# Stacked attention scores: head by head in five one-bank rounds, and earlier due times for the copies of the stacked parts

## The chip, the cores and the metric

One core of one Trainium2 chip runs the whole program. The metric is device time in microseconds of one execution; lower is better. Three runs of the kernel before gave 959.68, 962.39 and 964.31 us (median 962.39).

## The reference

Three layers follow one another, all in float32:

```python
# attention: q, k, v are [8 batches, 8 heads, 576, 64]; mask by blocks of 64
scores = q @ k.T / 8;  scores[block_i < block_j] = -1e9
attn = exp(scores - rowmax);  attn /= rowsum + 1e-9
x = (attn @ v)                     # -> [4608 tokens, 512]
# first layer: h = x @ w_in [512 x 2048];  g = h if h > 0 else exp(h) - 1;  x = g @ w_out
# second layer: logits = x @ phi [512 x 32]; softmax over tokens dispatches to 8 experts,
# softmax over slots combines their outputs -> [4608, 512]
```

Row block u of 128 queries needs only the keys 0 to 128(u+1), so a head has score pieces that are 128, 256, 384 and 512 wide, and a last one of 64 queries by 576 keys.

## The kernel before, in words

**Work.** The two heads of one batch that stand side by side are a pair: 32 pairs (`NPAIR`), four to a batch. The tokens form 36 tiles of 128. While pairs of later batches go through attention, tiles of earlier ones go through the layers (`moe_tile`: 48 matmuls L861 to L863 of 512 columns for a tile, then transposes by way of DRAM, `turned`, and routing, L906 and L972). Pairs from 9 on (`STACK`) use the stacked form that the change is about, 23 of them; they run between 215 and 760 us of the span.

**A stacked pair.** q and k come in transposed by 32x32 blocks and DVE finishes the turn (L532) into `QT[0]` and `KT[0]`, of which there is one copy. `pair_split` makes each head's stacked operands: ACT rounds q into `X1` (L555) and k into `Y` (L557), POOL forms the rests `KL` (L561) and `X2` (L566), and two DMAs a head copy `X1` and `KL` to the other 64 partitions (`qk_late<-qk_late`, four a pair). Operands of a head are one buffer, so those of the next pair wait for this pair's score matmuls.

**Scores.** `pair_scores` makes one fill after another in the two PSUM banks `SB0` and `SB0+512`. Piece `"b"` (the last 64 queries of both heads, L602) lies across both banks. Pieces `(u, h)` of row block u and head h go to bank h. Fill 1 is `(3,0)` and `(3,1)`, fill 2 `(2,0)`, `(0,0)` and `(2,1)`, `(0,1)`, fill 3 `(1,0)` and `(1,1)`: six bank loads a pair (L621). For each, DVE writes the mask (L629, L631) and takes the row maximum (L634), and ACT takes exp with the row sum (L637) into an SBUF area; that empties the bank.

**After the scores.** A pair is normalized in two halves, `HALVES`: `"b"` with fill 1, and fills 2 and 3. `pair_weights` takes the reciprocals (L649, L650) and POOL scales the pieces (L654). `pair_swap` transposes them: part by PE (L368) and part by DVE (L736), which then go to DRAM as one store (`swapped<-att`) and come back in six loads (`att<-swapped`). `swapped_values` multiplies by v (L786).

**What sets the order.** Every operation is given to `Plan.add` with an engine, an estimated duration, what it reads and writes, and a due time (`key`). `Plan.order` simulates the engines with these estimates, and on each engine takes the ready operation with the lowest key. What comes out is a fixed order for each engine; at run time each queue is followed strictly, and semaphores make it wait. Reads and writes are tracked there by named keys, while the framework below it also orders two engines' accesses to one PSUM bank in the order in which they were written out. SyncE (SP) issues all DMAs of this stretch from one queue (L363); the plan counts 0.48 us for each issue. Keys that matter here, with `base` the due time of a pair, 24 apart within a batch: scores `base + 4 fl`, halves of the weights and their swap `base + 7` and `base + 16`, loads of q and k `base - 30`, of v `base - 16`, preparation `base - 14` and some more. `turned` traffic of tile i has `22 i + 5.5 r + 0.5`.

Of the kernel before, what the change touches and what calls it, by code (L numbers as in the profile page):

```python
# [18 lines left out]
P = 128  # L19
# [15 lines left out]
MASKED = -1e9  # L35
# [204 lines left out]
def attention_moe_kernel(ctx: ExitStack, tc, q, k, v, w_in, w_out, phi, w1, w2, consts, out):  # L240
# [74 lines left out]
    def f(o, n, p0=0, p1=P):  # L315
        return view(as_f32, o, n, p0, p1)
# [7 lines left out]
    def pb(o, n, p0=0, p1=P):  # L324
        return ps[p0:p1, o:o + n]
# [218 lines left out]
    def pair_split(n, key):  # L544


        add("POOL", 0.64, lambda e: nc.gpsimd.tensor_scalar(
            out=f(QT[0], 512), in0=f(QT[0], 512), scalar1=SCALE, scalar2=0.0, op0=ALU.mult, op1=ALU.add), w=[("qt", 0)], key=key + 0.5)
        for h in range(2):
            here, there = (D * h, D * h + D), (D - D * h, P - D * h)  # L550
            x1, x2, y, kl = X1[h], X2[h], Y[h], KL

            def key_of(j):
                return [("stack", h, j)]
            add("ACT", 0.5, lambda e, x1=x1, here=here: nc.scalar.copy(st(x1, 512, *here), f(QT[0], 512, *here)),  # L555
                r=[("qt", 0)], w=key_of(0), key=key + 1)
            add("ACT", 0.5, lambda e, y=y, here=here: nc.scalar.copy(st(y, 512, *here), f(KT[0], 512, *here)),  # L557
                r=[("kt", 0)], w=key_of(1), key=key + 1)
            load(lambda x1=x1, there=there: st(x1, 512, *there, F32), lambda x1=x1, here=here: st(x1, 512, *here, F32), 200000,
                 r=key_of(0), w=key_of(2), key=key + 2, lag=TLAG)  # L560
            add("POOL", 1.35, lambda e, y=y, here=here: nc.gpsimd.tensor_tensor(  # L561
                out=st(KL, 512, *here), in0=f(KT[0], 512, *here), in1=st(y, 512, *here, F32), op=ALU.subtract),
                r=[("kt", 0)] + key_of(1), w=[("kl", h)], key=key + 2)
            load(lambda y=y, there=there: st(y, 512, *there, F32), lambda here=here: st(KL, 512, *here, F32), 200000,
                 r=[("kl", h)], w=key_of(3), key=key + 3, lag=TLAG)
            add("POOL", 1.47, lambda e, x1=x1, x2=x2, here=here: nc.gpsimd.tensor_tensor(  # L566
                out=st(x2, 512, *here), in0=f(QT[0], 512, *here), in1=st(x1, 512, *here, F32), op=ALU.subtract),
                r=[("qt", 0)] + key_of(0), w=key_of(4), key=key + 3)
# [3 lines left out]
    FILLS = (("b",), ((3, 0), (3, 1)), ((2, 0), (2, 1), (0, 0), (0, 1)), ((1, 0), (1, 1)))  # L572
    HALVES = (FILLS[0] + FILLS[1], FILLS[2] + FILLS[3])

    def pat(x, n):

        return PB + (PW[0] * (n % 2) + UNITS[x][1] if x in HALVES[0] else PW[0] + UNITS[x][1])

    def pkey(x, n):
        return ("p", x, n % 2 if x in HALVES[0] else 0)  # L580

    def wide(x):
        return S if x == "b" else P * (x[0] + 1)

    def pair_scores(n, fill, key):
        s = n % 2
        one = s if n < STACK else 0
        qt, kt = QT[one], KT[one]
        banks, bkeys = ((H0, H0 + 512), [("h", 0), ("h", 1)]) if n < 4 and fill % 2 else ((SB0, SB0 + 512), [("sb", 0), ("sb", 1)])
        units = FILLS[fill]  # L590

        def at(x):
            return banks[0] + 224 if x == "b" else banks[x[1]] + (384 if x[0] == 0 else 0)

        def keys(x):
            return bkeys if x == "b" else [bkeys[x[1]]]

        def sc(e):
            if fill == 0 and n >= STACK:
# [12 lines left out]
        cols = S if fill == 0 else sum(wide(x) for x in units) // 2  # L612
        last = fill == 0 and n >= STACK
        if n >= STACK and not last:
            for h in range(2):
                mine = [u for u, y in units if y == h]

                def st_sc(e, h=h, mine=mine):
                    for u in mine:
                        for x, first in ((X1, True), (X2, False)):  # L620
                            mm(pb(at((u, h)), P * (u + 1)), lhsT=st(x[h] + P * u, P), rhs=st(Y[h], P * (u + 1)), start=first, stop=not first)  # L621
                add("PE", sum(2 * (0.016 + P * (u + 1) / 2400) for u in mine), st_sc, r=[("stack", h, j) for j in range(6)], w=[bkeys[h]], key=key)
        else:
            add("PE", (0.0 if last else 0.15) + cols / 600, sc, r=([("qb", s, h) for h in range(3)] if last else [("qt", one)]) + [("kt", one)],
                w=bkeys, key=key, load=1.0, mode="F" if last else "R")
        for x in units:
            if n >= STACK and fill == 2 and x[0] == 2:
                both = pb(at(x) + 256, 256, 0, 64).rearrange("p (a y) -> p a y", a=2)[:, :, 64:]
                add("DVE", 0.14, lambda e, both=both: nc.vector.memset(both, MASKED), w=keys(x), key=key)  # L629
            elif x != "b" and not (n >= STACK and fill == 2):  # L630
                add("DVE", 0.11, lambda e, x=x: nc.vector.memset(pb(at(x) + P * x[0] + 64, 64, 0, 64), MASKED), w=keys(x), key=key)  # L631
        for x in units:
            c = nm_col + 9 * s + UNITS[x][0]
# [3 lines left out]
            add("ACT", 0.50 + wide(x) / 1300, lambda e, x=x, c=c: nc.scalar.activation(  # L637
                f(pat(x, n), wide(x)), pb(at(x), wide(x)), AF.Exp, bias=f(c, 1), scale=1.0,
                accum_out=f(sum_col + 9 * s + UNITS[x][0], 1)),
                r=keys(x) + [("nm", s, x)], w=[pkey(x, n), ("sum", s, fill // 2)], key=key)  # L640

    def pair_weights(n, half, key):
        s = n % 2
        units = HALVES[half]
        c0, nc_ = UNITS[units[0]][0], len(units)
        sm, rs = sum_col + 9 * s + c0, rs_col + 9 * s + c0

        def rec(e):
# [3 lines left out]
        for x in units:  # L652
            p = pat(x, n)
            add("POOL", (0.28 + wide(x) / 1050) * (1.3 if n < 8 else 1.0), lambda e, x=x, p=p: nc.gpsimd.tensor_scalar(  # L654
                out=f(p, wide(x)), in0=f(p, wide(x)), scalar1=f(rs_col + 9 * s + UNITS[x][0], 1), scalar2=0.0,
                op0=ALU.mult, op1=ALU.add), r=[("rs", s, half)], w=[pkey(x, n)], key=key)

        if n >= NTP:
# [65 lines left out]
    def pair_swap(n, half, key):  # L724
# [5 lines left out]
        for x in HALVES[half]:  # L730
# [9 lines left out]
        groups = ([("b", c) for c in range(4)], [((3, 0), 3), ((3, 1), 3), ("b", 4)]) if half == 0 else ([((0, 0), 0), ((0, 1), 0)],)  # L740
        for gi, blocks in enumerate(groups):
            g = gi + 2 * half
            tb, tk = (PVB, "pvb")
# [4 lines left out]
            add("PE", 0.02 + 0.108 * len(blocks), tr, r=[pkey(x, n) for x in {b[0]: 0 for b in blocks}] + ["con"], w=[tk], key=key, load=0.0)  # L748

            def evac(e, g=g, tb=tb):  # L750
                if g == 0:
# [269 lines left out]
    def tail(key):  # L1021
        qkk = [("stack", h, j) for h in range(2) for j in range(6)] + [("kl", h) for h in range(2)]
        att = [(nm, a) for nm in ("rq", "rk") for a in range(4)] + [(nm, 0) for nm in ("qt", "kt")] + [("qb", s, h) for s in range(2) for h in range(3)] + \
              [("v", s, j) for s in range(NV) for j in range(3)] + [pkey(x, s) for x in UNITS for s in range(2)] + \
# [223 lines left out]
    for n in range(NPAIR):  # L1248
        b, p = divmod(n, 4)
        base = T * 4.5 * (b - 1) + 24.0 * p - 24.0 - (min(EARLY, 8.0 + 4.0 * (n - NTP)) if n >= NTP else 0.0) if b else KAS * p + KA0  # L1250
        ev.append((base - (27 if n < STACK else KLD) if n < STACK else max(base - KLD, free + 0.1), lambda n=n, x=base - KLD: pair_load(n, x)))
        ev.append((before + 12.1 if n >= STACK else base - 14, lambda n=n, x=base - 14: pair_prep(n, x)))
        free = before + 12.1 if n >= STACK else base + 24 if n < NTP else free
        before = base
        ev.append((base - 16, lambda n=n, x=base - 16: pair_load_v(n, x)))
        for fl in range(4):
            ev.append((base + 4 * fl, lambda n=n, fl=fl, x=base + 4 * fl: pair_scores(n, fl, x)))
        for h in range(2):
            ev.append((base + 9 * h + 7, lambda n=n, h=h, x=base + 9 * h + 7: pair_weights(n, h, x)))
        ev.append((max(base + 24, T * 4.5 * (b - 1) + 0.1 if n >= NTP else -1e9), lambda n=n, x=base + 24: pair_values(n, x)))  # L1260
# [46 lines left out]
```

## Time and profile before

| | |
|---|---|
| median of 3 runs | 962.39 us |
| the profiled execution, its own time | 961.83 us |
| its span (first to last instruction) | 960.0 us |
| PE busy | 904.3 us (94%) |
| DVE busy | 693.4 us (72%) |
| ACT busy | 497.6 us (52%) |
| POOL busy | 392.5 us (41%) |
| mean granted TensorE clock | 0.989 |
| share of the chain that ended last | PE 59%, DVE 11%, DMA 11%, SP queue 7%, ACT 4%, POOL 3%, issue 3% |

An engine's busy time is the union of its instructions, so what is missing to the span is idle time. The chain that ended last is followed back from the last instruction, at each step to what released it. "a <- b" in a list of waits means that a stood idle and b's end let it go.

### The profile page before, as it was taken

What the parts mean: (1) busy time and instruction counts of PE and PEld (TensorE: products, weight loads), DVE (VectorE), ACT (ScalarE), POOL (GpSimd) and SP (SyncE); (2) the same over time, 40 slices, a digit from 0 to 9 for tenths busy, and PEclk for the clock granted to TensorE, in tenths of its full rate; (3) what the DMA queues carried; (4) which work ended last, traced back from release to release, by engine and by line L of the source; (5) the groups of instructions that cost most, each with busy time, mean ns of one, the idle gap of its engine ahead of it and who ended that gap; (6) DMA issues with size and microseconds to landing.
All of it is one profiled execution on the core that took longest, in us unless ns stands there. A gap on an engine that the chain in (4) does not pass through costs nothing.

```text
span 960.0 us, 20080 instructions
## 1 busy us (share of the span) xinstructions
PE 904.3 (94%) x6817; PEld 654.8 (68%) x6817; DVE 693.4 (72%) x1677; ACT 497.6 (52%) x1375; POOL 392.5 (41%) x519
## 2 busy tenths in 40 slices
PE   8898999999999999999999999999999999999992
PEld 6566777667676776776777777777777776766351
DVE  5896795578987897887879888788898844333150
ACT  5784655565555655555555555645555433322143
POOL 2874342147644555454635554455556210000000
PEclk9999999999999999999999999999999999999996
DMA  9946765248888887888977788878886788058959
GB/s 237 251 127 174 217 192 174 68 118 217 218 235 222 219 239 208 230 218 217 238 217 218 205 216 228 226 209 227 230 229 203 238 299 300 1 202 306 370 217 352
DMA packets 258551, 209.19 MB, mean 218 GB/s; under 512 B 182417, under 2 KB 205585, under 8 KB 255377
## 3 DMA queue, kind: packets, MB, share of 16 engines
q1 hardware_dynamic: 257248, 207.61, 75.0%
q8 instruction: 55, 0.90, 0.4%
q10 hardware_dynamic: 1200, 0.30, 0.1%
q14 instruction: 48, 0.39, 0.1%
HBM read 125.52 MB, written 70.25 MB: 204 GB/s over the span
## 4 chain that ended last, share of the span: by engine, by line
PE 59%; DVE 11%; DMA 11%; SPq 7%; ACT 4%; POOL 3%; issue 3%; ACTq 0%; DVEq 0%; POOLq 0%
PE ps L861 10%; PE ps L863 9%; PE ps L862 9%; PE ps L368 7%; SPq L363 7%; PE ps L786 4%; PE ps L621 4%; POOL att L654 3%; DMA att<-swapped 3%; PE ps L972 3%; PE ps L906 2%; PE ps L815 2%; DVE base L634 2%; ACT att L637 2%; PE ps L610 2%
## 5 line engine op out<-in xcount | busy, mean ns | idle before, releaser
L654 POOL TENSOR_SCALAR att<-att,base 128x128 f32<-128x128 f32 (+4 forms) x288 | 183.4, 654 | 197.6 <-DVE base L650 120.0
L861 PE MATMUL ps<-w,xhl 128*128 128x512 f32 x576 | 247.4, 430 | 0.0
L637 ACT ACTIVATE att<-ps,base 128x128 f32<-128x128 f32 (+4 forms) x288 | 157.7, 552 | 139.5 <-DVE base L634 124.7
L863 PE MATMUL ps<-w,xhl 128*128 128x512 f32 x576 | 226.8, 394 | 0.6 <-POOL xhl L843 0.6
L862 PE MATMUL ps<-w,xhl 128*128 128x512 f32 x576 | 225.8, 392 | 0.0
L634 DVE TENSOR_REDUCE base<-ps 128x1 f32<-128x128 f32 (+4 forms) x288 | 138.0, 502 | 17.5 <-PE ps L606 10.8
L861 PEld LDWEIGHTS ps<-w,xhl 128*128 128x128 f32 x576 | 108.8, 189 | 32.8 <-issue 14.4
L863 PEld LDWEIGHTS ps<-w,xhl 128*128 128x128 f32 x576 | 108.1, 188 | 25.9 <-POOL xhl L843 1.2
L862 PEld LDWEIGHTS ps<-w,xhl 128*128 128x128 f32 x576 | 109.0, 189 | 14.1
L344 ACT COPY att<-ps 128x512 f32<-128x512 f32 (+3 forms) x184 | 73.2, 437 | 64.5 <-PE ps L368 59.4
L566 POOL TENSOR_TENSOR qk_late<-att,qk_late 64x512 fp32r<-64x512 f32 x46 | 61.1, 1328 | 89.2 <-ACT qk_late L555 57.2
L786 PE MATMUL ps<-att 128*64 128x128 f32 (+2 forms) x960 | 74.5, 308 | 8.2 <-DMA att<-swapped 5.5
L621 PE MATMUL ps<-qk_late 128*128 128x512 f32 (+3 forms) x368 | 78.3, 328 | 2.3 <-ACT att L637 1.6
L843 POOL TENSOR_TENSOR xhl<-xe,xhl 128x512 fp32r<-128x512 f32 x36 | 46.6, 1296 | 82.6 <-ACT xhl L841 82.5
L368 PE MATMUL ps<-base,att 128*128 128x128 f32 x416 | 69.5, 279 | 10.0 <-POOL att L654 9.4
L621 PEld LDWEIGHTS ps<-qk_late 128*128 128x128 f32 x368 | 61.7, 188 | 22.2 <-ACT att L637 7.6
L786 PEld LDWEIGHTS ps<-att 128*64 128x64 f32 x960 | 49.6, 140 | 37.3 <-issue 26.6
L368 PEld LDWEIGHTS ps<-base,att 128*128 128x128 f32 x416 | 49.3, 142 | 36.0 <-POOL att L654 15.9
L736 DVE STREAM_TRANSPOSE att<-att 128x384 f32<-128x384 f32 x144 | 68.9, 502 | 0.5 <-POOL att L654 0.5
L868 DVE TENSOR_SCALAR g<-g 128x512 f32<-128x512 f32 x80 | 46.5, 581 | 28.9 <-ACT g L866 28.6
L866 ACT ACTIVATE g<-ps 128x512 f32<-128x512 f32 x80 | 47.4, 596 | 35.5 <-PE ps L863 33.5
L561 POOL TENSOR_TENSOR qk_late<-att,qk_late 64x512 fp32r<-64x512 f32 x46 | 60.2, 1308 | 2.3 <-ACT qk_late L557 1.1
(159 smaller groups left out, 1464.5 us busy)
## 6 DMA issues: line engine op xcount, KB each, us to landing
turned<-g SPq DMA_DIRECT2D x60, 512.0 KB, 3.4
swapped<-att SPq DMA_DIRECT2D x24, 1024.0 KB, 4.8
qk_late<-qk_late SPq DMA_DIRECT2D x92, 128.0 KB, 3.1
g<-turned SPq DMA_DIRECT2D x120, 96.0 KB, 2.7
att<-swapped SPq DMA_DIRECT2D x48, 192.0 KB, 4.0
att<-in_v_dram SPq DMA_DIRECT2D x64, 128.0 KB, 3.6
g<-in_moe_w_in_dram SPq DMA_DIRECT2D x16, 512.0 KB, 5.6
att<-in_moe_w_dram SPq DMA_DIRECT2D x8, 1024.0 KB, 10.2
```

What stands on the lines that cost most here:

```text
L344: nc.scalar.copy(o, i)
L363: (nc.sync if e == "SP" else nc.scalar).dma_start(out=o() if callable(o) else o, in_=i() if callable(i) else i)
L368: mm(o, lhsT=i, rhs=f(IDN + base, n, base, base + n), start=True, stop=True, is_transpose=True)
L621: mm(pb(at((u, h)), P * (u + 1)), lhsT=st(x[h] + P * u, P), rhs=st(Y[h], P * (u + 1)), start=first, stop=not first)
L634: add("DVE", 0.08 + wide(x) / 960, lambda e, x=x, c=c: nc.vector.tensor_reduce(out=f(c, 1), in_=pb(at(x), wide(x)), axis=AX.X, op=ALU.max, ...
L637: add("ACT", 0.50 + wide(x) / 1300, lambda e, x=x, c=c: nc.scalar.activation(f(pat(x, n), wide(x)), pb(at(x), wide(x)), AF.Exp, bias=f(c, ...
L654: add("POOL", (0.28 + wide(x) / 1050) * (1.3 if n < 8 else 1.0), lambda e, x=x, p=p: nc.gpsimd.tensor_scalar(out=f(p, wide(x)), in0=f(p, w ...
L736: add("DVE", 0.12 + P * cs / 960, lambda e, x=x, o=o, cs=cs: nc.vector.transpose(out=o, in_=f(pat(x, n), P * cs).rearrange("p (c m i) -> p ...
L786: mm(pb(o, w, 64 * h, 64 * h + 64), lhsT=f(vs + 320 * h + D * c, D), rhs=rhs(h), start=start, stop=stop)
L861: mm(pb(bank, 512), lhsT=fr(xh + P * kk, P), rhs=hi, start=(kk == 0), stop=False)
L862: mm(pb(bank, 512), lhsT=fr(xh + P * kk, P), rhs=lo, start=False, stop=False)
L863: mm(pb(bank, 512), lhsT=fr(xl + P * kk, P), rhs=hi, start=False, stop=(kk == 3))
```

## The change

The pairs from 9 on get a layout of their own. Pieces go head by head in five rounds after `"b"`, each in one bank, the banks in turn: `(3,0)`; `(2,0)` with `(0,0)`; `(1,0)` with `(1,1)`; `(3,1)`; `(2,1)` with `(0,1)`. Each round waits only for the stacked operands of the heads that it uses. The due times of the rounds are 4, 5.5, 8, 9.5 and 12 after `base`. The first half is now `"b"` and the first two rounds, the second half the last three. `(1,0)` and `(1,1)` lie beside each other in one bank and get one mask instruction instead of two. The transposes by PE are grouped to fit (still three groups of 4, 3 and 2 blocks). The due times of the two copies of a head go from `key + 2` and `key + 3` to `key - 8`. Preparation of the next pair is entered at 13.1 instead of 12.1 after `base`, behind the last round.

```diff
@@ pair_split
             load(lambda x1=x1, there=there: st(x1, 512, *there, F32), lambda x1=x1, here=here: st(x1, 512, *here, F32), 200000,
-                 r=key_of(0), w=key_of(2), key=key + 2, lag=TLAG)
+                 r=key_of(0), w=key_of(2), key=key - 8, lag=TLAG)
...
             load(lambda y=y, there=there: st(y, 512, *there, F32), lambda here=here: st(KL, 512, *here, F32), 200000,
-                 r=[("kl", h)], w=key_of(3), key=key + 3, lag=TLAG)
+                 r=[("kl", h)], w=key_of(3), key=key - 8, lag=TLAG)
@@
+    UNITS2 = {"b": (0, 0), (3, 0): (1, 640), (2, 0): (2, 1152), (0, 0): (3, 1536), (1, 0): (4, 1664), (1, 1): (5, 1920),
+              (3, 1): (6, 2176), (2, 1): (7, 2688), (0, 1): (8, 3072)}
+    FILLS2 = (("b",), ((3, 0),), ((2, 0), (0, 0)), ((1, 0), (1, 1)), ((3, 1),), ((2, 1), (0, 1)))
+    HALVES2 = (FILLS2[0] + FILLS2[1] + FILLS2[2], FILLS2[3] + FILLS2[4] + FILLS2[5])
@@ pair_scores
+        late = n >= STACK
+        units = FILLS2[fill] if late else FILLS[fill]
+        mine = (fill - 1) % 2
 
         def at(x):
+            if late and x != "b":
+                return banks[mine] + (384 if x[0] == 0 else 256 if x == (1, 1) else 0)
...
-            for h in range(2):
-                mine = [u for u, y in units if y == h]
-
-                def st_sc(e, h=h, mine=mine):
-                    for u in mine:
-                        for x, first in ((X1, True), (X2, False)):
-                            mm(pb(at((u, h)), P * (u + 1)), lhsT=st(x[h] + P * u, P), rhs=st(Y[h], P * (u + 1)), start=first, stop=not first)
-                add("PE", ..., st_sc, r=[("stack", h, j) for j in range(6)], w=[bkeys[h]], key=key)
+            def st_sc(e):
+                for u, h in units:
+                    for x, first in ((X1, True), (X2, False)):
+                        mm(pb(at((u, h)), P * (u + 1)), lhsT=st(x[h] + P * u, P), rhs=st(Y[h], P * (u + 1)), start=first, stop=not first)
+            add("PE", ..., st_sc,
+                r=[("stack", h, j) for h in sorted({y for _, y in units}) for j in range(6)], w=[bkeys[mine]], key=key)
...
-            elif x != "b" and not (n >= STACK and fill == 2):
+            elif late and x == (1, 0):
+                both = pb(at(x), 512, 0, 64).rearrange("p (a y) -> p a y", a=2)[:, :, 192:]
+                add("DVE", 0.14, lambda e, both=both: nc.vector.memset(both, MASKED), w=keys(x), key=key)
+            elif x != "b" and not (late and (x[0] == 0 or x == (1, 1))):
@@ pair_swap
+            groups = ([("b", c) for c in range(4)], [((0, 0), 0), ((3, 0), 3), ("b", 4)]) if half == 0 else ([((0, 1), 0), ((3, 1), 3)],)
@@ the events
-        ev.append((before + 12.1 if n >= STACK else base - 14, lambda n=n, x=base - 14: pair_prep(n, x)))
+        ev.append((before + 13.1 if n >= STACK else base - 14, lambda n=n, x=base - 14: pair_prep(n, x)))
...
-        for fl in range(4):
-            ev.append((base + 4 * fl, lambda n=n, fl=fl, x=base + 4 * fl: pair_scores(n, fl, x)))
+        for fl in range(4 if n < STACK else 6):
+            x = base + (4 * fl if n < STACK else (0, 4, 5.5, 8, 9.5, 12)[fl])
+            ev.append((x, lambda n=n, fl=fl, x=x: pair_scores(n, fl, x)))
```

## Rows read from the trace of the kernel before

**Rows 1.** Busy time by stretch: stretch, length, PE, PEld, DVE, ACT, POOL, clock, DMA

```profile
560.00:660.00 100.00, 94.99 (x689) 72.78 (x682) 82.67 (x207) 53.31 (x152) 50.59 (x69) 0.98 0.82 222
660.00:760.00 100.00, 99.78 (x750) 76.12 (x751) 86.32 (x222) 55.95 (x164) 52.98 (x69) 1.00 0.79 218
sum 545.00, PE 525.90 PEld 399.33 DVE 463.04 ACT 303.59 POOL 292.34; mean PE 87.65 PEld 66.56 DVE 77.17 ACT 50.60 POOL 48.72
...
900.00:960.00 60.00, 40.33 (x303) 19.25 (x295) 17.58 (x28) 21.82 (x42) 0.00 (x0) 0.85 0.83 305
```

**Rows 2.** Waits of PE, 205 to 790 us: us in total, times, longest

```profile
PE ps L786 <- DMA att<-swapped: 5.5, 5, 1.8
PE ps L368 <- ACT base L949: 4.0, 3, 2.0
PE ps L786 <- DMA g<-turned: 2.5, 2, 1.8
PE ps L368 <- ACT base L942: 1.7, 1, 1.7
PE ps L906 <- DMA g<-turned: 1.7, 2, 1.1
PE ps L621 <- ACT att L637: 1.6, 3, 1.2
...
PE ps L621 <- DMA qk_late<-qk_late: 0.4, 1, 0.4
```

**Rows 3.** Groups by line and form, 205 to 790 us: busy, mean ns, idle before

```profile
L634 DVE TENSOR_REDUCE base<-ps 128x1 f32<-128x256 f32 x48 | 18.9, 409 | 0.4
...
L634 DVE TENSOR_REDUCE base<-ps 128x1 f32<-128x128 f32 x48 | 12.4, 273 | 3.3 <-ACT att L637 3.1
...
L631 DVE MEMSET ps<- 64x64 f32 x95 | 10.2, 112 | 13.7 <-PE ps L621 12.2 <-ACT g L866 0.5
...
L629 DVE MEMSET ps<- 64x128 f32 x46 | 7.5, 165 | 6.0 <-PE ps L621 3.6 <-ACT att L637 1.8
```

**Rows 4.** PE in order of time, around the scores of three pairs: start, length

```profile
300.09 0.64 PE L621 MATMUL ps<-qk_late 128*128 128x256 f32 x4
300.56 0.40 PE L861 MATMUL ps<-w,xhl 128*128 128x512 f32 x1
...
304.65 1.13 PE L602 MATMUL ps<-att 128*128 128x288 f32 x4
...
312.72 1.17 PE L621 MATMUL ps<-qk_late 128*128 128x512 f32 x4
...
346.20 0.40 PE L621 MATMUL ps<-qk_late 128*128 128x256 f32 x2
346.44 0.40 PE L861 MATMUL ps<-w,xhl 128*128 128x512 f32 x1
```

**Rows 5.** ACT, POOL and SP in order of time, preparation of one pair

```profile
300.45 0.62 ACT L555 CAST qk_late<-att 64x512 fp32r<-64x512 f32 x1 [0.63 <-issue]
...
309.75 0.74 ACT L637 ACTIVATE att<-ps,base 128x576 f32<-128x576 f32 x1 [1.25 <-DVE base L634]
...
302.41 2.64 POOL L561 TENSOR_TENSOR qk_late<-att,qk_late 64x512 fp32r<-64x512 f32 x2
...
303.75 2.85 SPq L363 DMA_DIRECT2D att<-swapped  x6
306.70 1.12 SPq L363 DMA_DIRECT2D qk_late<-qk_late  x2
...
308.54 1.64 SPq L363 DMA_DIRECT2D qk_late<-qk_late  x2
```

**Rows 6.** DMA issues of the page: count, size, us to landing

```profile
qk_late<-qk_late SPq DMA_DIRECT2D x92, 128.0 KB, 3.1
```

**Rows 7.** ACT and DVE in order of time, two pieces of one bank

```profile
319.43 0.58 ACT L637 ACTIVATE att<-ps,base 128x384 f32<-128x384 f32 x1 [0.57 <-POOL att L654]
...
320.13 0.95 DVE L634 TENSOR_REDUCE base<-ps 128x1 f32<-128x128 f32 x3 [0.63 <-ACT att L637]
```

More of the change, by code (lines that the diff above doesn't have):

```diff
@@ L573, in attention_moe_kernel, with units_of, halves_of @@
     HALVES = (FILLS[0] + FILLS[1], FILLS[2] + FILLS[3])
+    UNITS2 = {"b": (0, 0), (3, 0): (1, 640), (2, 0): (2, 1152), (0, 0): (3, 1536), (1, 0): (4, 1664), (1, 1): (5, 1920),
+              (3, 1): (6, 2176), (2, 1): (7, 2688), (0, 1): (8, 3072)}
+    FILLS2 = (("b",), ((3, 0),), ((2, 0), (0, 0)), ((1, 0), (1, 1)), ((3, 1),), ((2, 1), (0, 1)))
+    HALVES2 = (FILLS2[0] + FILLS2[1] + FILLS2[2], FILLS2[3] + FILLS2[4] + FILLS2[5])
+    def units_of(n):
+        return UNITS if n < STACK else UNITS2
+    def halves_of(n):
+        return HALVES if n < STACK else HALVES2
     def pat(x, n):
-        return PB + (PW[0] * (n % 2) + UNITS[x][1] if x in HALVES[0] else PW[0] + UNITS[x][1])
+        o = units_of(n)[x][1]
+        return PB + (PW[0] * (n % 2) + o if x in halves_of(n)[0] else PW[0] + o)
     def pkey(x, n):
-        return ("p", x, n % 2 if x in HALVES[0] else 0)
+        return ("p" if n < STACK else "p2", x, n % 2 if x in halves_of(n)[0] else 0)
     def wide(x):
@@ L586, in pair_scores @@
         s = n % 2
+        if n == STACK and fill == 0:
+            for m in range(2):
+                handover([pkey(x, STACK + m) for x in HALVES2[0]], [pkey(x, STACK + m - 2) for x in HALVES[0]])
+            handover([pkey(x, STACK) for x in HALVES2[1]], [pkey(x, STACK - 1) for x in HALVES[1]])
         one = s if n < STACK else 0
@@ L589, in pair_scores @@
         banks, bkeys = ((H0, H0 + 512), [("h", 0), ("h", 1)]) if n < 4 and fill % 2 else ((SB0, SB0 + 512), [("sb", 0), ("sb", 1)])
-        units = FILLS[fill]
+        late = n >= STACK
+        units = FILLS2[fill] if late else FILLS[fill]
+        mine = (fill - 1) % 2
         def at(x):
+            if late and x != "b":
+                return banks[mine] + (384 if x[0] == 0 else 256 if x == (1, 1) else 0)
             return banks[0] + 224 if x == "b" else banks[x[1]] + (384 if x[0] == 0 else 0)
         def keys(x):
-            return bkeys if x == "b" else [bkeys[x[1]]]
+            return bkeys if x == "b" else [bkeys[mine if late else x[1]]]
         def sc(e):
@@ L614, in pair_scores @@
         if n >= STACK and not last:
-            for h in range(2):
-                mine = [u for u, y in units if y == h]
-                def st_sc(e, h=h, mine=mine):
-                    for u in mine:
-                        for x, first in ((X1, True), (X2, False)):
-                            mm(pb(at((u, h)), P * (u + 1)), lhsT=st(x[h] + P * u, P), rhs=st(Y[h], P * (u + 1)), start=first, stop=not first)
-                add("PE", sum(2 * (0.016 + P * (u + 1) / 2400) for u in mine), st_sc, r=[("stack", h, j) for j in range(6)], w=[bkeys[h]], key=key)
+            def st_sc(e):
+                for u, h in units:
+                    for x, first in ((X1, True), (X2, False)):
+                        mm(pb(at((u, h)), P * (u + 1)), lhsT=st(x[h] + P * u, P), rhs=st(Y[h], P * (u + 1)), start=first, stop=not first)
+            add("PE", sum(2 * (0.016 + P * (u + 1) / 2400) for u, _ in units), st_sc,
+                r=[("stack", h, j) for h in sorted({y for _, y in units}) for j in range(6)], w=[bkeys[mine]], key=key)
         else:
@@ L626, in pair_scores @@
         for x in units:
-            if n >= STACK and fill == 2 and x[0] == 2:
+            if late and x != "b" and x[0] == 2:
                 both = pb(at(x) + 256, 256, 0, 64).rearrange("p (a y) -> p a y", a=2)[:, :, 64:]
                 add("DVE", 0.14, lambda e, both=both: nc.vector.memset(both, MASKED), w=keys(x), key=key)
-            elif x != "b" and not (n >= STACK and fill == 2):
+            elif late and x == (1, 0):
+                both = pb(at(x), 512, 0, 64).rearrange("p (a y) -> p a y", a=2)[:, :, 192:]
+                add("DVE", 0.14, lambda e, both=both: nc.vector.memset(both, MASKED), w=keys(x), key=key)
+            elif x != "b" and not (late and (x[0] == 0 or x == (1, 1))):
                 add("DVE", 0.11, lambda e, x=x: nc.vector.memset(pb(at(x) + P * x[0] + 64, 64, 0, 64), MASKED), w=keys(x), key=key)
         for x in units:
-            c = nm_col + 9 * s + UNITS[x][0]
+            c = nm_col + 9 * s + units_of(n)[x][0]
             add("DVE", 0.08 + wide(x) / 960, lambda e, x=x, c=c: nc.vector.tensor_reduce(
@@ L638, in pair_scores @@
                 f(pat(x, n), wide(x)), pb(at(x), wide(x)), AF.Exp, bias=f(c, 1), scale=1.0,
-                accum_out=f(sum_col + 9 * s + UNITS[x][0], 1)),
-                r=keys(x) + [("nm", s, x)], w=[pkey(x, n), ("sum", s, fill // 2)], key=key)
+                accum_out=f(sum_col + 9 * s + units_of(n)[x][0], 1)),
+                r=keys(x) + [("nm", s, x)], w=[pkey(x, n), ("sum", s, fill // (3 if late else 2))], key=key)
     def pair_weights(n, half, key):
         s = n % 2
-        units = HALVES[half]
-        c0, nc_ = UNITS[units[0]][0], len(units)
+        units = halves_of(n)[half]
+        c0, nc_ = units_of(n)[units[0]][0], len(units)
         sm, rs = sum_col + 9 * s + c0, rs_col + 9 * s + c0
@@ L654, in pair_weights @@
             add("POOL", (0.28 + wide(x) / 1050) * (1.3 if n < 8 else 1.0), lambda e, x=x, p=p: nc.gpsimd.tensor_scalar(
-                out=f(p, wide(x)), in0=f(p, wide(x)), scalar1=f(rs_col + 9 * s + UNITS[x][0], 1), scalar2=0.0,
+                out=f(p, wide(x)), in0=f(p, wide(x)), scalar1=f(rs_col + 9 * s + units_of(n)[x][0], 1), scalar2=0.0,
                 op0=ALU.mult, op1=ALU.add), r=[("rs", s, half)], w=[pkey(x, n)], key=key)
@@ L729, in pair_swap @@
             handover(swap_keys(0) + swap_keys(1), [x for y in range(NPT) for x in pt_keys[y]])
-        for x in HALVES[half]:
+        for x in halves_of(n)[half]:
             if x == "b" or x[0] == 0:
@@ L739, in pair_swap @@
         both = f(py, 2 * YW).rearrange("p (h w) -> p h w", h=2)
-        groups = ([("b", c) for c in range(4)], [((3, 0), 3), ((3, 1), 3), ("b", 4)]) if half == 0 else ([((0, 0), 0), ((0, 1), 0)],)
+        if n < STACK:
+            groups = ([("b", c) for c in range(4)], [((3, 0), 3), ((3, 1), 3), ("b", 4)]) if half == 0 else ([((0, 0), 0), ((0, 1), 0)],)
+        else:
+            groups = ([("b", c) for c in range(4)], [((0, 0), 0), ((3, 0), 3), ("b", 4)]) if half == 0 else ([((0, 1), 0), ((3, 1), 3)],)
         for gi, blocks in enumerate(groups):
@@ L750, in evac @@
             def evac(e, g=g, tb=tb):
-                if g == 0:
+                if g and n >= STACK:
+                    copy(e, f(py + YW * (g - 1), 640).rearrange("p (a x) -> p a x", x=320)[:, :, 0:P],
+                         pb(tb, 256).rearrange("p (a x) -> p a x", x=P))
+                    if g == 1:
+                        copy(e, both[:, :, 512:576], pb(tb + 256, P).rearrange("p (h x) -> p h x", h=2))
+                elif g == 0:
                     src = pb(tb, 512).rearrange("p (c h x) -> p h c x", c=4, h=2)
@@ L1023, in tail @@
         att = [(nm, a) for nm in ("rq", "rk") for a in range(4)] + [(nm, 0) for nm in ("qt", "kt")] + [("qb", s, h) for s in range(2) for h in range(3)] + \
-              [("v", s, j) for s in range(NV) for j in range(3)] + [pkey(x, s) for x in UNITS for s in range(2)] + \
+              [("v", s, j) for s in range(NV) for j in range(3)] + [pkey(x, s) for x in UNITS2 for s in range(NPAIR - 2, NPAIR)] + \
               [x for s in range(NPT) for x in pt_keys[s]] + swap_keys(0) + swap_keys(1) + [k for _, k in gmore[NG:]]
@@ L1251, in attention_moe_kernel @@
         ev.append((base - (27 if n < STACK else KLD) if n < STACK else max(base - KLD, free + 0.1), lambda n=n, x=base - KLD: pair_load(n, x)))
-        ev.append((before + 12.1 if n >= STACK else base - 14, lambda n=n, x=base - 14: pair_prep(n, x)))
-        free = before + 12.1 if n >= STACK else base + 24 if n < NTP else free
+        ev.append((before + 13.1 if n >= STACK else base - 14, lambda n=n, x=base - 14: pair_prep(n, x)))
+        free = before + 13.1 if n >= STACK else base + 24 if n < NTP else free
         before = base
         ev.append((base - 16, lambda n=n, x=base - 16: pair_load_v(n, x)))
-        for fl in range(4):
-            ev.append((base + 4 * fl, lambda n=n, fl=fl, x=base + 4 * fl: pair_scores(n, fl, x)))
+        for fl in range(4 if n < STACK else 6):
+            x = base + (4 * fl if n < STACK else (0, 4, 5.5, 8, 9.5, 12)[fl])
+            ev.append((x, lambda n=n, fl=fl, x=x: pair_scores(n, fl, x)))
         for h in range(2):
```

## The prediction

> **What bounds the kernel now.** I read first the busy time by stretch. The change touches only the stacked pairs, which run from 215 to 760 us, and there PE is busy 525.90 of 545.00 us [rows 1]: 19.1 us are idle, and these are all that a better order can take from PE, since no matmul goes or comes. In the last hundred microseconds of the stretch PE is busy 99.78 of 100.00, so the 19 us lie before 660. DVE, at 463.04, is the next engine, 82 us free. The 19.7 us that PE lacks after 900 belong to the last layers, which the change leaves alone.
>
> Then the waits of PE, which say what ended the idle time [rows 2]. Eight microseconds (5.5 and 2.5, seven waits) stand ahead of L786, the product with v, whose weights come back late through the swap; two of them are put down to `g<-turned`, a neighbour in the same queue. Another 5.7 us (4.0 and 1.7) stand ahead of the turn in the routing, which waits for exps of ACT that have nothing to do with pairs. 1.7 us are waits of L906 for turned tiles. The score rounds themselves account for 2.0 us: 1.6 for an exp that frees a bank, 0.4 for a stacked copy. So what the change works on directly holds PE for 2 of 962 us.
>
> Last I followed one pair's preparation through ACT, POOL and SP, because a shorter loop could act without a wait of its own.
>
> **The change part by part.** I work against the profiled execution's 961.83 us, 0.56 under the median of the runs.
>
> *Score matmuls.* The same 16 matmuls per pair, on the same columns. Splitting or joining them costs PE nothing: four of 256 columns in one block take from 300.09 to 300.56, 0.47 us, and a block of two takes 0.24 (346.20 to 346.44), twice that is 0.48 [rows 4]. So five rounds instead of six bank loads: 0 us. Bounds: a change to other work ahead of each block could cost or save about 0.1 us, as the four matmuls show that listed 0.64 and advanced 0.47; times 23 pairs, 2 us either way.
>
> *Masks.* Two masks of 0.112 us (L631) become one like L629's, 0.165, per pair [rows 3]: DVE is relieved of 23 x (0.224 - 0.165) = 1.4 us. DVE is not the bound, PE work hides it: 0 us.
>
> *Copies moved forward in SP's queue.* In the pair prepared at 300.45 the first cast of head 0 was done near 301.07, but copies left at 306.70 and 308.54, behind six loads of the swap that began at 303.75 [rows 5]. Are they now moved past those loads? By the keys, no: the loads there are of the pair two before in the queue, due 16 after that pair's `base`, which is 32 before the `base` of the pair prepared; the copies go from 12 or 11 before it to 22 before it, still behind. Loads of v at 16 before are passed, but are long issued; loads of q and k of the following pair were behind already. What is passed is the traffic of the tiles (`turned`), whose key is the current time. Each pair's four copies can put 4 x 0.48 (two in 1.12, two in 1.64: 0.56 to 0.82 each) = 2 to 3 us ahead of some turned load. PE waits for turned loads at L906 in only two places, 1.7 us in 23 pairs [rows 2]. Bounds: -1.7 if these go too, +1.9 x 23 = +44 if every routing were hit. I take 0, by the row that shows 1.7.
>
> *Earlier first round.* Round 1 needs head 0 only. Its rest is done one 1.32 us step after 302.41 [rows 5], near 303.7; with an issue of about 0.5 and 3.1 us to landing [rows 6] its operands stand at 307.4. Before, fill 1 followed at 312.72 [rows 4]. Of these 5.3 us most is not to be had: `"b"` covers both banks, its matmuls come at 304.65, and its exp ran from 309.75 to 310.49, itself after a DVE that got to it late. Round 1 can start near 310.7, 2.0 us earlier: what is late next is the drain of `"b"`. In the waits this shows as 1.6 us for the exp against 0.4 us for the copy [rows 2]. PE had other work meanwhile, so the gain on the path is what it waited: -0.4 to -2.0; I take -1.0.
>
> *Halves and swap.* Both halves keep their columns (1600 and 1536); the second has five pieces instead of six, so a little less fixed work stands between the last exp and the store. The next pair's head 0 may be cast after round 3, while rounds 4 and 5 still run. Both let L786's operands come a little sooner relative to PE's place for them. Bounds: from none of the 8.0 us gone (or 8 more, if the new order places L786 earlier than the swap lands) to all gone. I take -1.5, nearer to none, because the issue order of the swap's own DMAs against the copies is as before.
>
> *Clock.* After the wait of 1.8 us ahead of an L786 the granted clock of 560 to 660 was 0.98 [rows 1], about 2 us lost at the lower of the two levels, 1.2 instead of 2.4 GHz, in part of that stretch. If that wait shrinks this goes as well; bounds -2 to +2, I take -0.8.
>
> Sum: 961.83 - 1.0 - 1.5 - 0.8 = 958.5 us.
>
> **The rivals.**
>
> *A, forecast: small gain, 953 to 963.* For it: the work of PE unchanged, 2.0 us of direct waits, the rest only reshuffled.
>
> *B, the idle time goes.* A looser loop lets the order always have something ready, and 215 to 660 becomes like 660 to 760, where PE lacked 0.2 us in 100 [rows 1]. Then about 16 of the 19 us and the 2 us of clock go: 944 to 950. For it: the copies of one pair left 5 us after their cast [rows 5], and the heads now overlap. Against it: 5.7 us of the waits are routing on ACT, and `"b"` still takes both banks.
>
> *C, slower: the shared bank.* Pieces of one round now share a bank with nothing of the other bank between them. Today, where DVE's maximum of `(0,h)` shares a bank with ACT's exp of `(2,h)`, it stood idle 0.63 us until the exp that began at 319.43 had ended [rows 7]; in all 3.1 us before the 48 maxima of 128 columns [rows 3], because the maximum of `(2,1)`, in the other bank, lies between. If the order puts the second maximum behind the first exp, DVE is held in three rounds of each pair: 3 x 23 x 0.63 = 43 us of its 82 free. The bank is then released 0.6 us late and exps of the tiles queue behind. It decides from the point where PE has nothing else: some ten such rounds beyond the three in which it waits today give 6 us, twenty 13 us; 965 to 973. Against it: at equal keys the plan runs both maxima back to back, so that only the first exp waits 0.27 or 0.41 us for the second [rows 3], which costs ACT, half idle, nothing that PE sees.
>
> This one has a page. The Trainium skill, "PSUM — Partial Sum Buffer", section "PSUM bank collisions raise a hardware error", says that two engines may not be in one bank and partition quadrant at the same time, two readers included, and asks for a semaphore by bank. The trace agrees: the 0.63 us are such a wait, of one reader for another. By the rule alone, pieces with a bank each, as `(1,0)` and `(1,1)` had, are the better layout, and the time would be that of C.
>
> *D, no effect.* The drain of `"b"`, not the copies, sets the first round, and the new order only moves the 19 us about: 960 to 965. For it: the later pairs run with PE full already.
>
> **How the numbers follow.** A 0.45, B 0.17, D 0.20, C 0.18. The runs before span 0.5%, and about that, 4.8 us (below 957.6, above 967.2), is what a measurement can tell. A lies half on either side of the first line, more above it: 0.20 faster, 0.25 same. B is faster, 0.17. D is the same but for 0.02 slower and 0.01 faster. C is slower but for 0.02. Faster 0.38, same 0.44, slower 0.18. The likeliest case's own range is 953 to 963; to hold 8 in 10 it must reach into B and C: 948 to 968.
>
> **What would show it.** L621's waits for `qk_late<-qk_late` gone and those for ACT L637 still there: the step on the first round holds. First L621 of a pair following the exp of `"b"` by a few tenths: `"b"` is the gate. DVE's idle time ahead of 128-column maxima under 1 us: C is out; over 20 us: C holds. Issues of copies directly after casts, with waits of L906 for `turned` grown: the copies displace tiles. PE's idle time from 215 to 660 is the test of the sum: some 16 us by A, under 5 by B, over 25 by C. The forecast is wrong if PE's busy time in the stretch moves by more than 3 us, since I hold its work to be the same, or if the waits ahead of L786 more than halve or double.

## The result and the profile after

The changed kernel takes 967.39 us (median of 10 runs, 965.77 to 970.74), the kernel before 961.75 (10 runs, 959.41 to 965.45). The ratio is 1.0052, 95% interval 1.0028 to 1.0077: slower by 5.6 us, a little over what can be told from no change. The forecast was 958.5. The profiled execution of the changed kernel, 970.74 us, is the slowest of its ten, so the two profiles lie further apart than the medians.

Lines moved by the edit: L621 is now L638, L602 is L622, L634 is L655, L637 is L658, L786 is L815, L906 is L935, L949 and L942 are L978 and L971.

**Where the two traces part.** PE's order is the same in both until the third stacked score matmul. The first starts at 222.39 us before and at 224.92 after, so 2.5 us of the profile's difference in span (968.6 to 960.0) arise where both do the same; the clock goes with it: between 50 and 100 us it stood at 1.00 before and at 0.93 after. From the first stacked score matmul to the end (busy time by stretch: length, PE, PEld, DVE, ACT, POOL, clock, DMA), first the kernel before:

```profile
222.39:960.05 737.66, 696.41 (x5233) 506.23 (x5231) 530.24 (x1281) 363.19 (x1010) 294.42 (x391) 0.99 0.79 231
...
50.00:100.00 50.00, 45.34 (x370) 31.17 (x370) 40.53 (x88) 32.07 (x84) 25.17 (x25) 1.00 0.59 156
```

and the changed kernel, with its stretches that answer to [rows 1]:

```profile
224.92:968.62 743.70, 697.93 (x5233) 505.76 (x5231) 518.10 (x1266) 360.92 (x1002) 294.25 (x391) 0.98 0.79 229
...
50.00:100.00 50.00, 44.38 (x359) 30.74 (x356) 37.73 (x82) 29.44 (x78) 26.48 (x25) 0.93 0.53 145
...
215.00:760.00 545.00, 523.43 (x3864) 396.54 (x3861) 448.53 (x1105) 301.89 (x866) 293.72 (x395) 0.99 0.82 220
560.00:660.00 100.00, 95.45 (x719) 72.38 (x718) 80.74 (x202) 54.33 (x158) 51.99 (x69) 0.98 0.82 225
660.00:760.00 100.00, 96.97 (x733) 73.69 (x732) 82.88 (x208) 55.87 (x158) 51.54 (x70) 1.00 0.80 218
```

The same 5233 matmuls take 6.0 us longer. PE's idle time is length less busy time: 41.3 us before, 45.8 after. That is 4.5 of the 6.0; the other 1.5 are busy time, longer at the lower clock. Within 215 to 760 idle time went from 19.1 to 21.6, and the hundred microseconds before 760, full before, now lack 3.0. From 215 to 660, where all of it was looked for, it is 18.5, before 18.9.

The waits of PE, 205 to 790 us, the answer to [rows 2]:

```profile
PE ps L368 <- ACT base L971: 6.0, 6, 1.6
PE ps L815 <- DMA att<-swapped: 4.0, 4, 2.0
PE ps L935 <- DMA g<-turned: 2.3, 3, 1.0
PE ps L815 <- DMA g<-turned: 2.2, 2, 1.4
PE ps L368 <- ACT xe L344: 2.0, 1, 2.0
PE ps L368 <- ACT base L978: 1.7, 4, 0.8
PE ps L638 <- ACT att L658: 1.4, 2, 1.1
PE ps L368 <- DVE att L346: 1.1, 2, 0.9
PE ps L622 <- ACT att L658: 0.7, 1, 0.7
```

No single wait carries the loss. Waits ahead of the product with v fell from 8.0 to 6.2 us. Those of the routing's turn rose from 5.7 to 7.7. Transposes now wait 3.1 us for evictions L344 and L346, which stood at none of these places before.

**What the change did to a pair.** PE and ACT in order of time, one pair and the casts of the next:

```profile
508.99 1.14 PE L622 MATMUL ps<-att 128*128 128x288 f32 x4
512.72 1.13 PE L638 MATMUL ps<-qk_late 128*128 128x512 f32 x6
515.83 0.64 PE L638 MATMUL ps<-qk_late 128*128 128x256 f32 x4
520.74 1.25 PE L638 MATMUL ps<-qk_late 128*128 128x512 f32 x6
...
511.02 0.74 ACT L658 ACTIVATE att<-ps,base 128x576 f32<-128x576 f32 x1 [1.23 <-DVE base L655]
516.19 0.62 ACT L555 CAST qk_late<-att 64x512 fp32r<-64x512 f32 x1 [0.79 <-issue]
521.92 0.62 ACT L555 CAST qk_late<-att 64x512 fp32r<-64x512 f32 x1 [0.25 <-PE ps L638]
```

Head 0 of the next pair is cast at 516.19, while rounds 4 and 5 are still to come at 520.74; before, the cast at 300.45 came behind the last fill at 300.09 [rows 4, 5]. Worked out over the 23 pairs (start of the first to end of the last score matmul of a pair), the rounds take 8.8 us in the median, 11.6 before, and the first comes 3.6 us after the last copy of its pair has landed, 0.8 before. So the change does what it says: the loop is looser. PE got no more done for it: from the first stacked score matmul to the end of the last it is 534.4 us, before 537.5, but 26 fewer matmuls of the tiles are done by then, some 6 us of PE at the 0.23 us at which they follow one another.

**The shared bank** (groups of DVE's maxima, as in [rows 3]):

```profile
L655 DVE TENSOR_REDUCE base<-ps 128x1 f32<-128x256 f32 x48 | 18.9, 417 | 2.0 <-ACT att L658 1.2
...
L655 DVE TENSOR_REDUCE base<-ps 128x1 f32<-128x128 f32 x48 | 13.1, 274 | 1.1 <-ACT att L658 1.1
```

DVE stood idle ahead of 128-column maxima for 1.1 us, before 3.3, and with those of 256 columns for 3.1, before 3.7: rival C is out.

### The profile page after: what moved, and what is told of

It is laid out like the page before. It is cut to its first block, busy times and chain, and to the rows that moved or that the text cites. A ratio compares the mean times of both kernels' runs of the same rounds, so it can differ in the third digit from the quotient of the medians.

```text
span 968.6 us, 20058 instructions
## 1 busy us (share of the span) xinstructions
PE 907.4 (94%) x6817; PEld 655.7 (68%) x6817; DVE 680.0 (70%) x1662; ACT 495.2 (51%) x1367; POOL 392.4 (41%) x519
## 4 chain that ended last, share of the span: by engine, by line
PE 69%; DVE 8%; DMA 7%; SPq 6%; ACT 4%; issue 2%; POOL 2%; ACTq 0%; DVEq 0%; POOLq 0%
PE ps L890 11%; PE ps L892 10%; PE ps L891 10%; PE ps L368 8%; PE ps L815 7%; SPq L363 6%; PE ps L638 4%; PE ps L1001 3%; PE ps L935 2%; PE ps L622 2%; POOL att L675 2%; DMA att<-swapped 2%; PE ps L1302 2%; PE ps L844 2%; DVE base L655 2%
## 5 line engine op out<-in xcount | busy, mean ns | idle before, releaser
L675 POOL TENSOR_SCALAR att<-att,base 128x512 f32<-128x512 f32 (+4 forms) x288 | 184.2, 657 | 210.3 <-DVE base L671 174.7
L658 ACT ACTIVATE att<-ps,base 128x512 f32<-128x512 f32 (+4 forms) x288 | 157.8, 552 | 104.1 <-DVE base L655 99.6
L655 DVE TENSOR_REDUCE base<-ps 128x1 f32<-128x512 f32 (+4 forms) x288 | 138.2, 505 | 16.1 <-PE ps L626 10.7
L344 ACT COPY att<-ps 128x256 f32<-128x256 f32 (+3 forms) x178 | 71.4, 442 | 64.3 <-PE ps L368 60.0
L815 PE MATMUL ps<-att 128*64 128x128 f32 (+2 forms) x960 | 74.0, 308 | 6.2 <-DMA att<-swapped 4.0
L638 PE MATMUL ps<-qk_late 128*128 128x256 f32 (+3 forms) x368 | 74.9, 325 | 1.4 <-ACT att L658 1.4
L815 PEld LDWEIGHTS ps<-att 128*64 128x64 f32 x960 | 49.3, 140 | 35.0 <-issue 23.6
L638 PEld LDWEIGHTS ps<-qk_late 128*128 128x128 f32 x368 | 61.6, 188 | 16.4 <-ACT att L658 3.8
L757 DVE STREAM_TRANSPOSE att<-att 128x384 f32<-128x384 f32 (+1 forms) x144 | 69.0, 506 | 2.4 <-POOL att L675 2.2
L908 DVE STREAM_TRANSPOSE g<-g 128x512 f32<-128x512 f32 x84 | 57.8, 692 | 0.7
```

Source lines behind the costliest of these rows:

```text
L344: nc.scalar.copy(o, i)
L815: mm(pb(o, w, 64 * h, 64 * h + 64), lhsT=f(vs + 320 * h + D * c, D), rhs=rhs(h), start=start, stop=stop)
```

## The experiments

Two theories had a mechanism: the copies pushed ahead displace tile traffic ("copies"), or the five one-bank rounds cost time ("rounds"). The third had none in the change itself: any other fixed order, whatever brought it about, finds PE's work and its operands at other moments, and PE's idle time is dealt anew ("redraw"). All were timed in five rounds beside the kernel before. In the table idle time is worked out as above, from the first stacked score matmul to the end; it is that of one profiled execution, the ratio that of the runs.

**The two parts, each alone.**

```diff
# e1_copies_only: the kernel before, and
-                 r=key_of(0), w=key_of(2), key=key + 2, lag=TLAG)
+                 r=key_of(0), w=key_of(2), key=key - 8, lag=TLAG)
-                 r=[("kl", h)], w=key_of(3), key=key + 3, lag=TLAG)
+                 r=[("kl", h)], w=key_of(3), key=key - 8, lag=TLAG)
# e2_rounds_only: the changed kernel, and these two lines put back
```

> The kernel before with only the due times of the stacked copies moved to key - 8; layout, rounds and halves as before. Theory 'copies' (the copies pushed ahead displace tile traffic on SP, and that is the loss): 965 to 970, ratio 1.004 to 1.009, waits of PE for g<-turned clearly above the 4.2 us of before. Theory 'rounds' (the five one-bank rounds are the loss): 959 to 963, ratio near 1.000. Theory 'redraw' (no part costs anything by itself, each new order only redraws PE's idle time): anywhere from 957 to 970, with PE's idle time redistributed over unrelated waits.

> The changed kernel with the due times of the copies put back to key + 2 and key + 3; rounds, halves and packing as changed. Theory 'copies': back to 959 to 963, ratio near 1.000. Theory 'rounds': stays at 965 to 970, ratio 1.004 to 1.009. Theory 'redraw': anywhere from 957 to 970, and the two parts' losses (this one and the copies alone) do not add up to the 5.6 us of both.

The copies alone: ratio 1.0046 (1.0029 to 1.0063). The rounds alone: 1.0025 (1.0005 to 1.0045). Each theory claimed one of them near 1.000, and neither is, the rounds alone narrowly. The parts add to 0.7% where both together cost 0.5%, which their intervals allow: that the prices add is not excluded by this. One reserve: in the order of e1 the program's output is 3.3% off the reference, for a cause that is not known, and nothing below rests on e1 alone. The waits of the copies alone (205 to 900 us) bear displaced tile traffic out only in small part:

```profile
PE ps L786 <- DMA att<-swapped: 4.4, 3, 2.5
PE ps L786 <- DMA g<-turned: 4.2, 4, 1.8
...
PE ps L906 <- DMA g<-turned: 1.5, 3, 0.8
```

What is put down to `g<-turned` rose from 4.2 to 5.7 us, as "copies" had it, but all of the rise stands ahead of the product with v; routing waited 1.5 us for turned tiles, before 1.7. The two waits of the product with v give 8.6, before 8.0. That is little of the 5.6 us by which PE's idle time grew.

**Orders that differ by due times alone.**

```diff
# e3_shift_before: the kernel before; e5, e9, e10 shift the same times by 0.25, 1.0, 2.0
-  ev.append((base + 4 * fl, lambda n=n, fl=fl, x=base + 4 * fl: pair_scores(n, fl, x)))
+  ev.append((base + 4 * fl, lambda n=n, fl=fl, x=base + 4 * fl + (0.5 if n >= STACK and fl else 0.0): pair_scores(n, fl, x)))
# e4_shift_after: the changed kernel; e7, e11 shift the same times by 0.5, -0.25
-  ev.append((x, lambda n=n, fl=fl, x=x: pair_scores(n, fl, x)))
+  ev.append((x, lambda n=n, fl=fl, x=x + (0.25 if n >= STACK and fl else 0.0): pair_scores(n, fl, x)))
```

> The kernel before, with nothing changed but that the three stacked fills after b are due 0.5 later on the planner's scale; no operation is added, removed, resized or moved to another engine. Theories 'copies' and 'rounds': no change, 960 to 964, ratio 0.998 to 1.002, since neither mechanism is touched. Theory 'redraw': the order of about 2800 lines on PE differs, and the time moves by 2 to 8 us in either direction, because the order of the kernel before is one good draw.

> The changed kernel, with nothing changed but that its five rounds are due 0.25 later on the planner's scale. Theories 'copies' and 'rounds': the same as the changed kernel, 965 to 970. Theory 'redraw': moves by 2 to 8 us against the changed kernel, in either direction.

> The kernel before with the three stacked fills due 0.25 later: a change of the same kind as the shift by 0.5, but small enough that the fixed orders on PE and SP come out the same as before, and only a few neighbours on DVE, ACT and POOL change places. Theory 'redraw' (what costs is another fixed order): 960 to 965, ratio 0.998 to 1.002. If instead the time rises by over 0.3% here too, it is not the order that costs but something in the shift itself.

The shift by 0.5 in the kernel before: ratio 1.0081 (1.0052 to 1.0109), no less than the change itself. The changed kernel shifted by 0.25: 1.0109 (1.0085 to 1.0132). The control, whose orders on PE, SP and POOL are those of before, with a few neighbours swapped on DVE and ACT: 0.9995 (0.9972 to 1.0018). So the cost comes with another order, not with the shift. From the first stacked score matmul to the end, e3 and then the control:

```profile
221.92:967.60 745.68, 697.30 (x5233) 506.55 (x5231) 531.42 (x1278) 365.50 (x1013) 294.85 (x391) 0.99 0.79 228
...
223.46:959.90 736.44, 693.97 (x5233) 504.64 (x5231) 529.93 (x1281) 363.05 (x1010) 294.40 (x391) 0.99 0.79 231
```

**SP's queue alone.** Here the orders of the four compute engines are held fixed, and copies are moved forward by hand:

```diff
# e6_sp_only: the kernel before, in the last lines; `order` is the plan's, with its times
...
+        for c in marks["copies"]:
+            at = next(j for j, x in enumerate(order) if x[1] == c)
+            ready = max(ends[d] for d in plan.ops[c][3] if d in ends) + 0.15
+            first = next(j for j, x in enumerate(order) if x[0] >= ready)
+            first = max(first, 1 + max(j for j, x in enumerate(order[:at]) if x[1] in plan.ops[c][3]))
+            if first < at:
+                order.insert(first, (ready,) + order.pop(at)[1:])
...
```

> The kernel before with the orders of PE, DVE, ACT and POOL kept as they are; in SP's queue alone each stacked copy is moved forward to where its producer has just ended by the plan, ahead of whatever stood between. Theory 'copies' (the copies ahead displace tile and swap traffic by up to 2 us per pair and that reaches PE): 966 to 972, ratio 1.004 to 1.010, with more waits of PE for g<-turned and att<-swapped than the 9.7 us of before. Theory 'redraw': 960 to 966, ratio 0.998 to 1.003, since PE's order, fitted to the old landings, has the same work at the same places and few of its waits depend on 1 or 2 us of these DMAs.

By the plan's times 18 of the 92 copies had something to pass and stand one to six places further forward; the orders of the other four engines are those of before. Ratio 1.0016 (0.9988 to 1.0044): not told from no change; the range of "copies", 1.004 to 1.010, is only just reached by the upper end. Its waits (220 to 900 us), in an execution of 958.27 us, the fastest of its twelve:

```profile
PE ps L786 <- DMA att<-swapped: 4.0, 3, 1.8
...
PE ps L786 <- DMA qk_late<-qk_late: 1.9, 1, 1.9
...
PE ps L621 <- ACT att L637: 1.6, 3, 1.2
PE ps L906 <- DMA g<-turned: 1.6, 3, 0.7
```

Once a copy now stands last ahead of a product with v, for 1.9 us, and the waits put down to the swap are lower, 4.0 us against 5.5. Moving the copies ahead is by itself worth between -1.2 and +4.2 us by this.

**More orders of both layouts.**

```diff
# e8_due_after: the changed kernel; e12_rounds_due: the same with the copies' due times of before
-            x = base + (4 * fl if n < STACK else (0, 4, 5.5, 8, 9.5, 12)[fl])
+            x = base + (4 * fl if n < STACK else (0, 4, 4, 8, 8, 12)[fl])
```

> The changed kernel with its five rounds due 0.5 later. Theory 'redraw': another draw, 960 to 976, not near the 974.5 of the shift by 0.25 by any rule. Theory 'later rounds cost' (the shift by 0.25 cost 0.6% against the changed kernel because rounds come late): above 974.

> The changed kernel with the due times 0, 4, 4, 8, 8, 12, the ones that the kernel before has for its fills. Theory 'rounds spread out' (the times 5.5 and 9.5 in between break the rounds into more blocks and that costs): 959 to 964. Theory 'redraw': anywhere from 960 to 976.

> The kernel before with the three stacked fills due 1.0 later: a third order of the old layout. Theory 'redraw, and the old order was a picked one': slower than before again, ratio 1.002 to 1.012, as the new layout's orders are. Rival 'the old layout is better by itself': the old layout's orders centre on the time of before, so this one is as likely below as above, ratio 0.996 to 1.004.

> The kernel before with the three stacked fills due 2.0 later: a fourth order of the old layout. The same two theories: ratio 1.002 to 1.012 by 'redraw, and the old order was a picked one', 0.996 to 1.004 by 'the old layout is better by itself'.

> The changed kernel with its five rounds due 0.25 earlier: another order of the new layout. By 'redraw' the new layout's orders scatter as the old one's do, ratio to before 1.002 to 1.012. By 'the old layout is better by itself' they centre on the changed kernel's 1.005.

> The changed layout with the copies' due times of before and the due times 0, 4, 4, 8, 8, 12: the two single steps that came out cheapest in the new layout (1.0025 and 1.0044 against before), taken together. If steps had prices that add up, this would be the best of the new layout, 959 to 963. By 'redraw' their prices don't combine: ratio to before anywhere from 1.000 to 1.010.

| order | layout | ratio to before (95%) | PE idle, us | of it 660 to 760 |
|---|---|---|---|---|
| before | old | 1 | 41.3 | 0.2 |
| e5, same orders on PE and SP | old | 0.9995 (0.9972 to 1.0018) | 42.5 | 0.2 |
| e6, other order on SP alone | old | 1.0016 (0.9988 to 1.0044) | 40.7 | 0.5 |
| e1, copies ahead | old | 1.0046 (1.0029 to 1.0063) | 46.9 | 2.5 |
| e3, fills 0.5 later | old | 1.0081 (1.0052 to 1.0109) | 48.4 | 2.1 |
| e9, fills 1.0 later | old | 1.0050 (1.0032 to 1.0069) | 49.9 | 2.2 |
| e10, fills 2.0 later | old | 1.0141 (1.0111 to 1.0171) | 53.8 | 5.0 |
| the changed kernel | new | 1.0052 (1.0028 to 1.0077) | 45.8 | 3.0 |
| e2, copies as before | new | 1.0025 (1.0005 to 1.0045) | 47.1 | 3.5 |
| e4, rounds 0.25 later | new | 1.0109 (1.0085 to 1.0132) | 52.4 | 5.0 |
| e7, rounds 0.5 later | new | 1.0076 (1.0045 to 1.0106) | 50.8 | 5.2 |
| e8, rounds due 4, 4, 8, 8, 12 | new | 1.0044 (1.0023 to 1.0066) | 46.3 | 3.7 |
| e11, rounds 0.25 earlier | new | 1.0117 (1.0087 to 1.0147) | 54.0 | 2.0 |
| e12, e2 and e8 together | new | 1.0027 (1.0010 to 1.0044) | 45.3 | 2.7 |

Four other orders of the old layout cost 0.46 to 1.41%, mean 0.80. Seven orders of the new one cost 0.25 to 1.17%, mean 0.64. The layouts are not told apart by this; what stands out is the one order that the kernel before has. Between 660 and 760 us PE lacks 0.2 to 0.5 us in the three runs with PE's order of before and 2.0 to 5.2 in the eleven others; the control, then e3:

```profile
660.00:760.00 100.00, 99.80 (x756) 75.69 (x756) 86.56 (x221) 56.17 (x166) 51.18 (x67) 1.00 0.78 217
...
660.00:760.00 100.00, 97.93 (x738) 74.53 (x737) 86.11 (x216) 55.67 (x160) 52.21 (x69) 1.00 0.78 211
```

"The old layout is better by itself" isn't borne out: its own neighbours are as slow. "Later rounds cost" is out for the new layout: 0.25 earlier, 0.25 later and 0.5 later give 1.0117, 1.0109 and 1.0076. In the old layout only later fills were tried, so there it stays possible that the due times of before suit it better than later ones.

Prices that add up are not excluded. For e12 959 to 963 was expected, and it took 967.06 us beside a kernel before of 964.36. But against the changed kernel's 1.0052, e2 saves 0.27 points and e8 0.08; taken together that makes 1.0017, and e12 measured 1.0027 (1.0010 to 1.0044). Copies moved ahead come out dearer in all four comparisons, by 0.46 (e1), 0.27 (the changed kernel against e2), 0.17 (e8 against e12) and 0.16 points (e6), the last three within noise. A price of their own of some 0.2%, 2 us, may be among what the change cost; these runs can't tell it from the new orders.

The time goes with PE's idle time, and what idle time is made of changes from order to order. The waits of the dearest order of the old layout, e10 (220 to 900 us):

```profile
PE ps L786 <- DMA att<-swapped: 6.9, 6, 2.1
PE ps L621 <- ACT att L637: 5.7, 8, 1.5
PE ps L621 <- DMA qk_late<-qk_late: 5.3, 7, 1.3
PE ps L368 <- ACT base L942: 4.3, 5, 1.8
```

and of the dearest of the new layout, e11:

```profile
PE ps L935 <- DMA g<-turned: 8.1, 7, 2.3
PE ps L815 <- DMA att<-swapped: 7.3, 6, 2.8
PE ps L638 <- ACT att L658: 3.5, 2, 2.8
PE ps L368 <- ACT base L971: 3.4, 3, 1.5
```

In the one the score rounds wait 11.0 us for banks and copies, in the other the routing waits 8.1 for turned tiles. One thing seems to go with the layout: over 205 to 900 us, PE's waits ahead of all score matmuls are 2.3 to 11.2 us in the seven runs of the old layout and 0.3 to 4.3 in those of the new one, while the routing's waits for turned tiles are 0 to 2.6 in the old and 2.3 to 8.1 in the new. In the mean that is 4.6 against 2.2 and 1.4 against 5.3: the new layout loosens the score rounds, as was meant, and PE waits more for turned tiles instead.

## Why the prediction was wrong

*Score matmuls, 0 us: right.* PE's busy time from the first of them on went from 696.41 to 697.93, about what the second dip of the clock costs (last section).

*Masks, 0 us on the path: right.* Of the 12 us that DVE is busy less from there to the end, masks are 1.4, as reckoned (46 of 64 columns fewer, 23 of 128 more). No gain on PE goes with it.

*Copies ahead, 0 us: not contradicted,* with -1.2 to +4.2 us in e6, all other orders held. The waits for turned tiles rose by 0.6 us in the changed kernel, between the bounds and near what was taken; with the copies due as before, e2 has 6.2 there, so the copies are not what makes them.

*Earlier first round, -1.0: right in the wait, a fifth of it in size.* The wait for the copy, 0.4 before, is gone, and is in all five orders of the new layout with copies due earlier. Those for an exp that frees a bank stayed: 1.4 at L638 and 0.7 at L622, before 1.6 at L621 and 0.3 at L602. So 2.3 us became 2.1. That the drain of `"b"` would be the gate is not borne out: the first round starts 1.4 us behind the end of that exp in the median of the pairs, before 1.3, and within half a microsecond in 4 of 23. In most pairs neither copy nor bank held it, but its place in PE's order.

*Halves and swap, -1.5: near in size, and nothing shows that the edit did it.* 8.0 became 6.2; but over all orders these waits are 6.3 to 11.0 us in the old layout, without these edits, and 6.2 to 10.5 in the new one, with them.

*Clock, -0.8: wrong in sign.* The stacked pairs have two dips instead of one (last section); 1.5 us more.

*What failed is the premise of the sum,* said in case A as "the rest only reshuffled" and in D as "the new order only moves the 19 us about", and with it the reading that the 19 us lie before 660 because the stretch behind is full. I started from the idle time of before as if reordering kept it, and took off what the edits could take off. But 41.3 us is not what an order of this program costs on the average; the eleven other orders on PE lie between 45.3 and 54.0, and the full stretch before 760 is full in the order of before alone. The test that was named, idle time from 215 to 660, gave 18.5 us and missed the loss, which lies behind: 3.0 instead of 0.2 up to 760, and 2.1 more from there to the end. In the changed kernel it comes to 4.5 us of idle time and 1.5 of clock, net of what the edits gave, of which the waits show 0.2 us at the score rounds. Had another order been priced as a term by the three shifts of the old layout, which change no work, +4.8 to +13.6 us (0.50 to 1.41% of 962, mean 0.91), the forecast would have been slower, near 967. The bound of 8 us for L786 "if the new order places L786 earlier than the swap lands" was this term, named for one wait only and then left out of the sum.

*What stays open.* Why this order fits so well isn't shown. If the order of before were one of twelve drawn alike, it would be the lowest once in twelve; whether it was found by trying or the due times of before suit the chip's real durations better than their neighbours, no run here tells. How much of the 5.6 us is the new order and how much a price of the change itself is open too, as is why the new layout waits more for turned tiles; that an order alone can cost this much is shown. That the looser loop is worth something in an order fitted to it wasn't tried beyond these seven.

## What to carry to other kernels

Where a planner writes one fixed order for all engines and the main engine is 95% busy, an edit does two things: it changes the work, and it deals the whole order anew. Measure the second by itself, with a change of due times that touches no work, before the first is given any credit or blame; here half a unit of due time cost no less than the change. In a forecast, give the new deal a term of its own, and don't centre it on zero when the present order is better than its neighbours.

## What the runs showed of the hardware

Within the stacked pairs the clock fell at the two longest waits of PE in the changed kernel, and the work behind them ran at the lower level of 1.2 GHz for some 3 us. PE in order of time, the changed kernel and, in the last two lines, the kernel before:

```profile
306.66 2.74 PE L815 MATMUL ps<-att 128*64 128x384 f32 x36 [1.35 <-DMA att<-swapped]
...
403.39 0.87 PE L368 MATMUL ps<-base,att 128*128 128x128 f32 x3 [2.01 <-ACT xe L344]
...
576.52 4.40 PE L815 MATMUL ps<-att 128*64 128x384 f32 x36 [1.98 <-DMA att<-swapped]
...
479.82 0.33 PE L368 MATMUL ps<-base 128*128 128x128 f32 x1 [2.04 <-ACT base L949]
...
596.83 4.25 PE L786 MATMUL ps<-att 128*64 128x384 f32 x36 [1.81 <-DMA g<-turned]
```

The same 36 matmuls took 2.74 us after a wait of 1.35 and 4.40 after one of 1.98; around 403 the granted clock of the 50 us was 0.97. So the wait of 1.98 us cost 1.7 us on top. Its length alone does not decide: in the kernel before the clock fell at a wait of 1.81 us, with 4.25 us for 36 such matmuls, and at one of 2.04 it did not (1.00 from 450 to 500 us). What decides is not shown here; waits of the same total can differ in price.
